# A new order for the steps of a two-stage attention and token-mixing kernel

## The chip, the cores and the metric

The kernel runs on one core of a Trainium2 chip. The metric is the time of one execution in microseconds on the device, as the median of several runs. All inputs and the output lie in the device's memory (DRAM) as float32.

## The reference

Two attentions stand one behind the other, and a token-mixing layer behind them. There are 8 batches of 8 heads, 576 tokens, 64 elements per head, and 32 packed queries per head.

```python
def sm_attn(qq, kk, vv):
    s = scale * np.matmul(qq, kk.transpose(0, 1, 3, 2))
    s = s - np.max(s, axis=-1, keepdims=True)
    a = np.exp(s)
    a = a / (np.sum(a, axis=-1, keepdims=True) + 1e-09)
    return np.matmul(a, vv)
p_packed = sm_attn(p, k, v)              # 32 packed rows per head
attn = sm_attn(q, p_packed, p_packed)    # 576 rows per head
...
x = attn.transpose(0, 2, 1, 3).reshape(B, S, H * D)      # (8, 576, 512)
wq = x @ w_q                             # (8, 576, 64)
wk = x @ w_k
W_tok = scale * np.einsum('bsd,btd->bst', wq, wk)
mixed = np.einsum('bst,btd->bsd', W_tok, x)
return np.maximum(mixed, 0.0) @ w_out
```

## The kernel before

Every batch is handled by the same chain of small steps, and the batches overlap: while TensorE multiplies for one batch, the other engines prepare the next. Each step is a short Python function that records a few instructions. The step's number is the batch, a second number its part. The steps of a batch in the order of the data:

- LD.k, LD.v, LD.q: loads from DRAM that convert to bfloat16, issued on GpSimd's queue. They all share one queue and land in its order.
- KT and QV (VectorE): 32x32 block transposes of k and q. S1 (TensorE): scores of the packed queries, 32 small matmuls. X1 (ScalarE): exponentials, two halves. TE (VectorE): transposes of them. PV (TensorE): the product with v, with a column of ones that gives the row sum.
- RC, PP, PT (VectorE): reciprocal, normalised packed values (`pp`), their transpose. QK (TensorE) and QKE, QD: packed values times the weights w_k and w_q.
- S2 (TensorE), X2 (ScalarE): scores of the 576 queries against the 32 packed rows and their exponentials, in chunks. RS, RR (VectorE): row sums and reciprocals. AM: the mask product, exponentials times reciprocal, on GpSimd or VectorE. Its part 2 is the last 128 columns of each half (256 in all), part 3 the first four tiles (1024), parts 0 and 1 two tiles each (512).
- AT, AE: transposes of the result on TensorE, and their copy out of PSUM. WKQ, WE: the products with QK's result. GM, GE, Y, YE, MX, MR: the mixing, through the 64-wide middle. RL, RLF, RLR: relu out of PSUM. OT, OH: the product with w_out, four matmuls of 512 columns for each tile of 128 tokens. OE, OEF, OEH: copies out of PSUM. ST, STF, STH: stores. OT.b.4 handles the 64 left-over tokens of two batches.
- WARM: matmuls of a tile of zeros into a PSUM bank that nobody reads. WARM.n has n units of 128 columns.

One string, `ORDER`, lists all steps. Each word names the step, behind `@` its engine (A ScalarE, V VectorE, P GpSimd, S SyncE; TensorE without a letter) and behind `=` the PSUM banks that it writes. A loop at the end of the kernel records them in that order:

```python
with tc.manual_schedule():
    for item in ORDER.split():
        name, _, bk = item.partition("=")
        name, _, eng = name.partition("@")
        f = name.split(".")
        ...
            steps[f[0]](*[int(z) for z in f[1:]], eng,
                        bk[0] if bk and len(bk) == 1 else bk)
```

So each engine runs its own steps in the order of the string, and waits at a step until what it reads, and the buffer or bank that it writes, are free. Nothing else orders the engines among each other. In particular nothing ties the mask product of one engine to that of another.

The lines that the texts below name: S1 L282, X1 L293, PV L315, RC L319, PP L323, QK L336, S2 L373, X2 L378, RS L394, RR L399, AM L405, AT L414 and L419, WKQ L441 and L446, GM L467, Y L477, MX L492, MR L498, RL and RLR L503 (ScalarE) and L505 (VectorE), OT L540, OH L580, WARM L619; all block transposes share L237, and copies L128 (ScalarE), L130 (GpSimd) and L132 (VectorE).

Of the kernel before, what the change touches and what calls it, by code (L numbers as in the profile page):

```python
# [13 lines left out]
LD.N0@A LD.N1@S SET.warm@V SET.v0@V SET.aT0@V SET.aT1@V SET.aT2@V SET.idf@V LD.W0@A LD.W1@S SET.tab@A LD.h0
LD.g0 LD.v0 LD.r0 LD.q0 LD.k1 NC.0@V PX.0@V NC.1@A PX.1@V SET.aff@P SET.idb@V SET.v3@P KT.0.0@V SET.mask@P
WC.1@P WC.0@P LD.k2 SET.v1@P LD.v1 SET.v2@P KT.0.1@V WARM.4=0 WARM.22.128=0 S1.0=0,1,2,3 X1.0.1@A TE.0.1@V
X1.0.0@A TE.0.0@V WARM.8=4 PV.0.0=4,5 PV.0.1 RC.0@V PP.0.0@V PP.0.1@V LD.q1 PT.0@V WARM.6=6 QK.0=6 QKE.0@A
QV.0.0@V QV.0.1@V QD.0@P WARM.4=7 S2.0.2=2,3 X2.0.2@A RS.0.2@V RR.0.2@V S2.0.0=0,1 LD.v2 S2.0.1=4,5 X2.0.0@A
RS.0.0@V RR.0.0@V X2.0.1@A RS.0.1@V RR.0.1@V AM.0.2@P WARM.6=7 AT.0.2=7 AE.0.2@A AM.0.0@P WARM.5=6 AT.0.0=6
KT.1.2@V AM.0.1@P WARM.3=2 AT.0.1=7 AE.0.1@A AE.0.0@V WKQ.0.0=2,3 WKQ.0.2 WE.0.0@A LD.q2 WKQ.0.1 KT.2.2@V  # L20
S1.1=0,1,4,5 WE.0.1@A GM.0=6 X1.1.0@A TE.1.0@V GE.0@A WARM.2=7 Y.0=2,3 YE.0@V S1.2=0,1,6,7 MR.0=2,3 X1.1.1@A
TE.1.1@V MX.0.0=4,5 X1.2.0@A LD.O PV.1.0=0,1 TE.2.0@V PV.1.1 X1.2.1@A TE.2.1@V RC.1@V LD.k3 PP.1.0@V PP.1.1@V
# [1 line left out]
RS.1.2@V RR.1.2@V S2.1.1=2,3 X2.1.0@A RS.1.0@V RR.1.0@V WARM.1=6 PV.2.0=6,7 PV.2.1 X2.1.1@A RS.1.1@V RC.2@V
LD.v3 QD.1@P AM.1.2@P AT.1.2=4 RR.1.1@V AM.1.0@P WARM.5=5 AT.1.0=5 AM.1.1@P LD.k4 PP.2.0@V AE.1.2@A PP.2.1@V
PT.2@V QK.2=4 AE.1.0@A QKE.2@A QD.2@P QV.2.2@V LD.q3 LD.v4 AT.1.1=0 AE.1.1@A WKQ.1.0=2,3 WKQ.1.2 WKQ.1.1
WE.1.0@V S2.2.2=6,7 WE.1.1@A X2.2.2@A S2.2.3=4,5 X2.2.3@A GM.1=1 OT.0.0=2,3 GE.1@V Y.1=6,7 OT.0.1 YE.1@A
RS.2.4@V OE.0.0@A MR.1=0,1 MX.1.1=4,5 RLR.1@A RR.2.4@V OT.0.2=6,7 LD.q4 OT.0.3 KT.3.2@V AM.2.3@P OE.0.1@V
RL.1.1@A S1.3=2,3,0,1 X1.3.0@A AM.2.2@P OT.1.4=4 TE.3.0@V LD.k5 AT.2.2=5 X1.3.1@A TE.3.1@V AT.2.3=2 AE.2.3@V
LD.v5 MX.1.0=6,7 AE.2.2@V PV.3.0=0,1 PV.3.1 OEF.1.4@A WKQ.2.0=2,3 WKQ.2.1 RC.3@V PP.3.1@V RL.1.0@A WKQ.2.2  # L30
WE.2.2@A OT.1.2=4,5 OT.1.3 PP.3.0@V PT.3@V QK.3=6 OE.1.1@A LD.q5 KT.4.2@V S1.4=0,1,2,3 GM.2=7 OT.1.0=4,5
X1.4.1@A LD.k6 GE.2@A QKE.3@V X1.4.0@A QV.3.2@V TE.4.1@V Y.2=2,3 YE.2@A S2.3.2=6,7 X2.3.2@A S2.3.3=0,1
X2.3.3@A MX.2.0=2,3 TE.4.0@V RL.2.0@A MR.2=6,7 RLR.2@V OT.1.1 MX.2.1=6,7 RL.2.1@A OE.1.0@A PV.4.0=0,1 QD.3@P
PV.4.1 RS.3.4@V RR.3.4@V LD.v6 AM.3.3@P AM.3.2@P RC.4@V OT.2.0=2,3 OT.2.1 LD.q6 OE.2.0@A PP.4.0@V PP.4.1@V
PT.4@V QK.4=6 AT.3.3=7 QV.4.2@V AT.3.2=0 AE.3.2@A LD.k7 S2.4.2=4,5 AE.3.3@V X2.4.2@A S2.4.3=2,3 X2.4.3@A
KT.5.2@V WKQ.3.0=0,1 WKQ.3.1 WKQ.3.2 RS.4.4@V RR.4.4@V QKE.4@A WE.3.2@A S1.5=4,5,2,3 X1.5.1@A LD.v7 TE.5.1@V
OT.2.2=6,7 AM.4.3@P QD.4@P AM.4.2@P GM.3=0 X1.5.0@A TE.5.0@V GE.3@A OT.2.3 Y.3=2,3 YE.3@V PV.5.0=4,5 PV.5.1
HOLD.v7 MR.3=0,1 RC.5@V PP.5.1@V OE.2.1@A MX.3.0=2,3 PP.5.0@V PT.5@V MX.3.1=6,7 RLR.3@A RL.3.0@A OT.3.4=0
RL.3.1@A AT.4.2=1 AE.4.2@A OEF.3.4@A QV.5.2@V AT.4.3=5 AE.4.3@V ST.1.4@P QK.5=4 QKE.5@V QD.5@P S2.5.2=2,3
X2.5.2@A KT.6.2@V S2.5.3=6,7 X2.5.3@A HA.5@P WKQ.4.0=0,1 WKQ.4.2 LD.q7 WKQ.4.1 WE.4.2@A OT.3.0=2,3  # L40
S1.6=4,5,6,7 X1.6.0@A GM.4=0 GE.4@V TE.6.0@V LD.r7 OT.3.1 X1.6.1@A TE.6.1@V Y.4=0,1 OE.3.0@A RS.5.4@V RR.5.4@V
PV.6.0=4,5 YE.4@A PV.6.1 MX.4.0=6,7 RC.6@V RL.4.0@A PP.6.0@V AM.5.3@P PP.6.1@V PT.6@V MX.4.1=2,3 AM.5.2@P
OT.3.2=0,1 OT.3.3 RL.4.1@A QK.6=4 QKE.6@A QV.6.2@V ST.2.1 S2.6.2=6,7 X2.6.2@A S2.6.3=2,3 ST.3.4 MR.4=4,5
X2.6.3@A OE.3.1@V RLR.4@V KT.7.2@V AT.5.2=6 AE.5.2@A AT.5.3=7 OT.4.0=0,1 OT.4.1 AE.5.3@A WKQ.5.0=4,5 WKQ.5.2
OE.4.0@A ST.0.8@P WKQ.5.1 RS.6.4@V WE.5.2@A RR.6.4@V ST.3.0 ST.4.0 ST.1.8@P S1.7=2,3,6,7 X1.7.1@A AM.6.3@V
OT.4.2=0,1 GM.5=4 TE.7.1@V OT.4.3 AT.6.3=5 X1.7.0@A TE.7.0@V GE.5@A OE.4.1@A AM.6.2@P AT.6.2=4 ST.2.0 Y.5=6,7
YE.5@A ST.3.1 PV.7.0=2,3 QV.7.1@V AE.6.3@V QV.7.0@V AE.6.2@A QD.6@P PV.7.1 RC.7@V PP.7.0@V PP.7.1@V PT.7@V
MR.5=0,1 RLR.5@A MX.5.1=6,7 RL.5.1@A MX.5.0=4,5 RL.5.0@V WKQ.6.0=0,1 WKQ.6.1 WKQ.6.2 WE.6.2@A OT.5.4=2
OEF.5.4@A S2.7.1=6,7 ST.5.4 GM.6=3 GE.6@V X2.7.1@A RS.7.1@V RR.7.1@V S2.7.2=0,1 X2.7.2@A S2.7.0=4,5 QK.7=2
X2.7.0@A RS.7.0@V RR.7.0@V Y.6=6,7 YE.6@A OT.5.2=0,1 MX.6.1=4,5 QKE.7@A MX.6.0=6,7 AM.7.1@P RS.7.2@V RR.7.2@V  # L50
MR.6=2,3 OT.5.3 RLR.6@V RL.6.0@V RL.6.1@A OE.5.1@A ST.4.1 AM.7.0@P OT.5.0=2,3 AM.7.2@P AT.7.0=4 AE.7.0@A
AT.7.1=5 AE.7.1@V AT.7.2=6 AE.7.2@V OT.6.2=0,1 OEF.6.2@A QD.7@P WKQ.7.0=4,5 WKQ.7.2 WKQ.7.1 WE.7.0@A WE.7.1@A
STF.6.2 OT.6.0=6,7 OT.6.1 GM.7=0 OE.6.0@V OT.5.1 OE.5.0@V ST.5.1 GE.7@A Y.7=4,5 OT.6.3 OEF.6.3@V ST.6.0
# [599 lines left out]
```

## Time and profile before

| | us |
|---|---|
| median of 3 runs | 104.29 |
| lowest, highest | 104.27, 104.53 |
| span of the profiled execution, first to last instruction | 102.8 |

| engine | busy us | share of the span |
|---|---|---|
| TensorE matmuls (PE) | 92.7 | 90% |
| TensorE weight loads (PEld, beside PE) | 54.6 | 53% |
| VectorE (DVE) | 73.7 | 72% |
| ScalarE (ACT) | 65.0 | 63% |
| GpSimd (POOL) | 51.8 | 50% |

The profile gives the profiled execution's span and no other time of it; the timed runs are 1.5 us longer than the span. A timeline row reads: start, duration, engine, line, operation, tile written <- tiles read, shape, count, and in brackets the idle time of the engine just before it and what ended that. A waits or groups row adds such instructions up. In the windows, the columns are the busy time of PE, PEld, DVE, ACT and POOL with their counts, the granted TensorE clock, the DMA engines' share and GB/s. Line numbers of the changed kernel are two lower, as the string has two lines less.

### The profile page before, as it was taken

To read this page: it belongs to the slowest core of one execution; us is meant where nothing else is said; L and a number is where in the kernel's file an instruction comes from. 1 tells how busy PE (TensorE), PEld (TensorE's weight loads), DVE (VectorE), ACT (ScalarE), POOL (GpSimd) and SP (SyncE) were. 2 spreads that over 40 slices of the span, in tenths; PEclk is the share of its full clock that TensorE was granted. 3 is DMA by queue.
4 is the path that set the end of the run, shared out by engine and by line. 5 is a ranking of instruction groups with operands and counts; after the bars stand their busy time and mean duration, and the time that the engine had idled before them with its cause. 6 is when DMAs were issued, how large, how long until landed. Compare 5 with 4: busy or idle time off the path is not lost.

```text
span 102.8 us, 3593 instructions
## 1 busy us (share of the span) xinstructions
PE 92.7 (90%) x1536; PEld 54.6 (53%) x1536; DVE 73.7 (72%) x140; ACT 65.0 (63%) x111; POOL 51.8 (50%) x81
## 2 busy tenths in 40 slices
...
PEclk9999999999999999999999999999999999999999
...
GB/s 9 249 230 207 213 210 213 207 209 213 205 211 207 212 211 210 213 205 212 211 212 207 211 213 204 217 211 203 255 262 409 411 410 408 418 345 264 335 364 160
DMA packets 13279, 25.13 MB, mean 244 GB/s; under 512 B 1040, under 2 KB 6416, under 8 KB 13008
## 3 DMA queue, kind: packets, MB, share of 16 engines
...
q8 instruction: 12, 0.20, 0.7%
...
## 4 chain that ended last, share of the span: by engine, by line
PE 49%; DMA 21%; DVE 8%; POOL 7%; ACT 6%; issue 3%; SPq 1%; DVEq 0%; POOLq 0%; ACTq 0%
PE ps L540 26%; DMA q_sb<-in_q_dram 13%; DMA o<-in_moe_w_q_dram 8%; PE ps L373 4%; POOL a L405 4%; PE ps L315 3%; ACT e1T L293 3%; PE ps L419 3%; PE ps L446 3%; DVE rs L394 2%; PE ps L441 2%; PE ps L467 2%; PE ps L282 2%; ACT e L378 1%; DVE qT L237 1%
## 5 line engine op out<-in xcount | busy, mean ns | idle before, releaser
L540 PE MATMUL ps<-wout,relu 128*128 128x512 bf16 x124 | 30.6, 380 | 0.0
L405 POOL TENSOR_TENSOR a<-e,rr 128x256 bf16<-128x256 f32 (+2 forms) x18 | 19.5, 1099 | 17.9 <-DVE rr L399 7.0
L619 PE MATMUL ps<-o 128*128 128x128 f32 (+3 forms) x76 | 19.5, 401 | 1.2 <-DVE o L135 1.2
L540 PEld LDWEIGHTS <-relu 128*128 128x128 bf16 x124 | 10.7, 98 | 11.7 <-issue 1.1
L128 ACT ACTIVATE o<-ps 128x1024 f32<-128x1024 f32 (+2 forms) x13 | 11.3, 871 | 5.4 <-PE ps L540 5.2
L619 PEld LDWEIGHTS ps<-o 128*128 128x128 f32 x76 | 11.3, 209 | 5.2 <-issue 3.6
L503 ACT ACTIVATE relu<-ps 128x1024 bf16<-128x1024 f32 (+1 forms) x14 | 13.0, 968 | 1.1 <-PE ps L492 1.1
L293 ACT ACTIVATE e1T<-ps 128x576 bf16<-128x576 f32 x16 | 9.8, 656 | 5.8 <-PE ps L282 5.2
L378 ACT ACTIVATE e<-ps 128x256 f32<-128x256 f32 (+2 forms) x19 | 11.2, 623 | 2.7 <-PE ps L373 2.5
L394 DVE TENSOR_REDUCE rs<-e 128x16 f32<-128x512 f32 (+2 forms) x13 | 10.9, 840 | 2.3 <-ACT e L378 2.2
L237 DVE STREAM_TRANSPOSE kT<-k_sb 128x1152 uint32<-128x1152 uint32 (+1 forms) x9 | 11.1, 1230 | 1.9 <-DMA k_sb<-in_k_dram 1.9
L173 POOL DMA_DIRECT2D v_sb<-in_v_dram x16 | 10.0, 628 | 4.0 <-DMA v_sb<-in_v_dram 1.6
L237 DVE STREAM_TRANSPOSE qT<-q_sb 128x1152 uint32<-128x1152 uint32 (+1 forms) x10 | 11.0, 1108 | 0.1
L132 DVE COPY o<-ps 128x1024 f32<-128x1024 f32 (+2 forms) x7 | 6.8, 977 | 5.3 <-PE ps L540 2.7
L237 DVE STREAM_TRANSPOSE e<-e1T 128x288 uint32<-128x288 uint32 x16 | 7.4, 468 | 3.1 <-ACT e1T L293 2.7
L128 ACT ACTIVATE aT<-ps 128x128 bf16<-128x128 f32 (+2 forms) x11 | 5.0, 465 | 5.7 <-PE ps L419 3.3
L128 ACT ACTIVATE wkq<-ps 128x448 bf16<-128x448 f32 (+1 forms) x10 | 7.2, 730 | 1.8 <-PE ps L446 1.7
L315 PE MATMUL ps<-v_sb,e 64*64 64x192 bf16 x288 | 7.5, 245 | 0.8 <-DVE e L237 0.5
L315 PEld LDWEIGHTS <-e 64*64 64x64 bf16 x288 | 5.9, 107 | 2.6 <-DVE e L237 2.1
L373 PEld LDWEIGHTS <-qT 64*128 64x128 bf16 x320 | 5.4, 94 | 2.8 <-DVE qT L237 1.7
L373 PE MATMUL ps<-ppT,qT 64*128 64x64 bf16 x320 | 6.6, 190 | 0.2 <-DVE qT L237 0.2
L446 PE MATMUL ps<-aT,pqk 128*128 128x256 bf16 (+1 forms) x48 | 6.8, 246 | 0.0
...
## 6 DMA issues: line engine op xcount, KB each, us to landing
...
```

What stands on the lines that cost most here:

```text
L128: nc.scalar.activation(o, i, COPY)
L173: nc.gpsimd.dma_start(v_bufs[b % NL][halves(i), 0:7:2], src)
L237: nc.vector.transpose(o, i)
L293: nc.scalar.activation(e1T[:, x], T["s1", b][x].rearrange("a c m -> a m c"), EXP, scale=scale)
L315: nc.tensor.matmul(T["pv", b][halves(cc), i], lhsT, rhs, start=n == 0, stop=n == R - 1, skip_group_check=True)
L373: nc.tensor.matmul(ps[:, y, t - t0, i], lhsT, rhs, start=e == 0, stop=e == 1)
L378: nc.scalar.activation(e2[:, t0:t1].rearrange("a t (i y n) -> a y (t i) n", i=2, y=2), T["s2", b, c].rearrange("a y t i n -> a y (t i) n") ...
L394: nc.vector.tensor_reduce(rs[:, t0 * H:t1 * H], src, axis=AX, op=ADD)
L405: e.tensor_tensor(a2[:, t0:t1].rearrange("a t i (u l) -> a (t i u) l", l=L), e2v(b, c), T["rr", b][:, t0 * H:t1 * H].to_broadcast((P, (t1 ...
L503: nc.scalar.activation(o, i, RELU)
L540: nc.tensor.matmul(ps, lhsT, wout[:, j, :], start=j == 0, stop=j == NJ - 1)
L619: nc.tensor.matmul(bank(int(bk), [w]), warm[:, 0:P], rhs, start=True, stop=True)
```

## The change

Only `ORDER` changes. Its words are the same up to the end of batch 0's first half (S1, PV, QK of batch 0), apart from bank numbers; behind that, the steps of batches 0 to 7 stand in another order, 39 steps change between ScalarE, VectorE and GpSimd, and many write other PSUM banks. Six mask products move from GpSimd to VectorE (AM.1.1, 2.3, 3.2, 4.2, 5.2, 7.2) beside the one that is there already (AM.6.3). The WARM units behind S1.1 grow from 11 to 17. Of the loads, LD.k4 is issued earlier, LD.q6 and LD.v6 change places.

```diff
-X1.2.0@A LD.O PV.1.0=0,1 TE.2.0@V PV.1.1 X1.2.1@A TE.2.1@V RC.1@V LD.k3 PP.1.0@V PP.1.1@V
-PT.1@V MX.0.1=6,7 QV.1.2@V RLR.0@A QK.1=2 QKE.1@V RL.0.0@A WARM.3=3 S2.1.2=4,5 S2.1.0=0,1 RL.0.1@A X2.1.2@A
...
+GE.0@A X1.2.1@A TE.2.1@V X1.2.0@A Y.0=0,1 TE.2.0@V YE.0@A LD.k3 WARM.3=6 MX.0.0=6,7 WARM.2=4 MX.0.1=4,5 QV.1.2@V
+PT.1@V WARM.3=2 RL.0.0@A S2.1.2=2,3 S2.1.1=0,1 X2.1.2@A X2.1.1@A S2.1.0=6,7 RS.1.2@V LD.v3 LD.k4 RR.1.2@V QK.1=2
```

The first place is on TensorE, around MX of batch 0 (L492 before, L490 after). The names are `y_0` for the result of YE.0, `o_1_86` for the tile of zeros of the fillers, `e1_1` for the exponentials of batch 1. Before:

```order
L498 MATMUL ps_61<-wkq_0_363,y_0_429 128x64
L492 LDWEIGHTS y_0_429
L492 MATMUL ps_61<-wkq_0_363,y_0_429 128x512
L492 LDWEIGHTS y_0_429
L492 MATMUL ps_61<-wkq_0_363,y_0_429 128x512
L315 LDWEIGHTS e1_1_197
L315 MATMUL ps_61<-v_sb1_66,e1_1_197 64x192
```

After:

```order
L475 MATMUL ps_61<-pp_0_243,g_0_496 64x128
L617 MATMUL ps_61<-o_1_86 128x384
L490 LDWEIGHTS y_0_508
L490 MATMUL ps_61<-wkq_0_363,y_0_508 128x512
L490 LDWEIGHTS y_0_508
L490 MATMUL ps_61<-wkq_0_363,y_0_508 128x512
L617 MATMUL ps_61<-o_1_86 128x256
```

MX.0.0 stood between MR.0 and PV.1; now it stands behind PV.1, Y.0 and a filler of 3 units, with another of 2 units behind it.

The second place is on VectorE and GpSimd, at the mask products of batch 4: `rr_285` is the reciprocal RR.4.4, `e_1_197` the transposed exponentials TE.5, `y_...` YE.3, `a_1_329` the mask product. VectorE before:

```order
L399 RECIPROCAL rr_285<-rs_283 128x40
L237 STREAM_TRANSPOSE e_1_197<-e1T_194 128x9x32 x2
L486 TENSOR_SCALAR y_429<-ps 128x256
L319 RECIPROCAL rec_241<-ps 128x2
L323 SCALAR_TENSOR_TENSOR pp_245<-ps,rec_241,mask 128x128 x2
```

VectorE after:

```order
L397 RECIPROCAL rr_285<-rs_283 128x40
L235 STREAM_TRANSPOSE e_1_197<-e1T_194 128x9x32 x2
L403 TENSOR_TENSOR a_1_329<-e_0_83,rr_285 128x256
L484 TENSOR_SCALAR y_508<-ps 128x256
L317 RECIPROCAL rec_241<-ps 128x2
L321 SCALAR_TENSOR_TENSOR pp_245<-ps,rec_241,mask 128x128 x2
```

GpSimd before:

```order
L173 DMA v_sb_68<-in_v_dram 64x4x576 x2
L405 TENSOR_TENSOR a_1_329<-e_0_83,rr_285 128x1024
L130 COPY pqk_264<-pqk_264 128x2x64
L405 TENSOR_TENSOR a_1_329<-e_0_83,rr_285 128x256
L559 DMA out_dram<-orem_866 128x512
```

GpSimd after:

```order
L174 DMA k_sb_72<-in_k_dram 128x2x1152
L403 TENSOR_TENSOR a_1_329<-e_0_83,rr_285 128x1024
L171 DMA v_sb_68<-in_v_dram 64x4x576 x2
L128 COPY pqk_264<-pqk_264 128x2x64
L386 TENSOR_TENSOR h_0_1411<-e_1_84 128x640
```

The small product AM.4.2 left GpSimd's queue for VectorE's, where it stands between TE.5.1 and YE.3; the loads of v7 went behind AM.4.3.

The third place is on VectorE at the start of batch 7: `rec_240` is RC.7, `pp_244` PP.7, `qT_268` QV.7, `ppT_250` PT.7, `aT_80` AE.6.3. Before:

```order
L237 STREAM_TRANSPOSE qT_268<-q_sb_76 128x2x288
L132 COPY aT_80<-ps 128x2x512
L237 STREAM_TRANSPOSE qT_268<-q_sb_76 128x2x288
L319 RECIPROCAL rec_240<-ps 128x2
L323 SCALAR_TENSOR_TENSOR pp_244<-ps,rec_240,mask 128x128 x2
L237 STREAM_TRANSPOSE ppT_250<-pp_244 128x128
```

After:

```order
L235 STREAM_TRANSPOSE qT_268<-q_sb_76 128x2x288
L130 COPY aT_80<-ps 128x2x512
L317 RECIPROCAL rec_240<-ps 128x2
L321 SCALAR_TENSOR_TENSOR pp_244<-ps,rec_240,mask 128x128
L503 TENSOR_SCALAR rem_632<-ps 128x4x64
L321 SCALAR_TENSOR_TENSOR pp_244<-ps,rec_240,mask 128x128
L235 STREAM_TRANSPOSE qT_268<-q_sb_76 128x2x288
L235 STREAM_TRANSPOSE ppT_250<-pp_244 128x128
```

RLR.5 went between the two PP, and QV.7.0 between them and PT.7.

More of the change, by code (lines that the diff above doesn't have):

```diff
@@ L13 @@
 ORDER = """
[L14 to L22, printed above, removed]
-PT.1@V MX.0.1=6,7 QV.1.2@V RLR.0@A QK.1=2 QKE.1@V RL.0.0@A WARM.3=3 S2.1.2=4,5 S2.1.0=0,1 RL.0.1@A X2.1.2@A
@@ L24 @@
[L24 to L53, printed above, removed]
@@ L54 @@
-STF.6.3 YE.7@A ST.5.0 MR.7=6,7 RLR.7@A MX.7.0=4,5 RLF.7.0.1@A RLF.7.0.0@V MX.7.1=2,3 RLF.7.1.0@A OT.7.4=0
-OEF.7.4@A ST.7.4 RLF.7.1.1@V OT.7.1=6 OEF.7.1@V OT.7.0=7 STF.7.1 OT.7.2=1 OEF.7.0@A OH.7.0=0 STF.7.0 OEF.7.2@A
-STF.7.2 OEH.7.0@V STH.7.0 OH.7.1=5 OEH.7.1@A STH.7.1@A
+LD.N0@A LD.N1@S SET.warm@V SET.v0@V SET.aT0@V SET.aT1@V SET.aT2@V SET.idf@V LD.W0@A LD.W1@S SET.tab@A LD.h0 LD.g0
+LD.v0 LD.r0 LD.q0 LD.k1 NC.0@V PX.0@V NC.1@A PX.1@V SET.aff@P SET.idb@V SET.v3@P KT.0.0@V SET.mask@P WC.1@P WC.0@P
@@ new lines @@
+LD.k2 SET.v1@P LD.v1 SET.v2@P KT.0.1@V WARM.4=0 WARM.22.128=0 S1.0=0,1,2,3 X1.0.1@A TE.0.1@V X1.0.0@A TE.0.0@V
+WARM.8=4 PV.0.0=4,5 PV.0.1 RC.0@V PP.0.0@V PP.0.1@V LD.q1 PT.0@V WARM.6=6 QK.0=0 QKE.0@A QV.0.0@V QV.0.1@V QD.0@P
+WARM.4=6 S2.0.2=6,7 X2.0.2@A RS.0.2@V RR.0.2@V S2.0.0=2,3 LD.v2 S2.0.1=4,5 X2.0.0@A RS.0.0@V RR.0.0@V X2.0.1@A
+RS.0.1@V RR.0.1@V AM.0.2@P WARM.6=1 AT.0.2=0 AE.0.2@A AM.0.0@P WARM.5=1 AT.0.0=0 KT.1.2@V AM.0.1@P WARM.3=1
+AT.0.1=1 AE.0.1@A AE.0.0@V WKQ.0.0=6,7 WKQ.0.2 WE.0.0@A LD.q2 WKQ.0.1 KT.2.2@V S1.1=2,3,4,5 X1.1.1@A WARM.3=0
```

32 lines of the change are left out of this document (added).

## The prediction

> **What bounds the kernel now.** I read the page's busy line first, then the windows, then TensorE's timeline for its waits, then the chain for what released them.
>
> ```profile
> span 102.8 us, 3593 instructions
> PE 92.7 (90%) x1536; PEld 54.6 (53%) x1536; DVE 73.7 (72%) x140; ACT 65.0 (63%) x111; POOL 51.8 (50%) x81
> PEclk9999999999999999999999999999999999999999
> 70.00:80.00 10.00, 10.00 (x196) 6.23 (x194) 9.83 (x14) 8.95 (x15) 5.38 (x6) 1.00 1.12 291
> 80.00:90.00 10.00, 9.96 (x150) 6.00 (x143) 7.44 (x18) 8.45 (x17) 2.86 (x4) 1.00 1.02 411
> ```
>
> TensorE is busy in 90% of the span, and in 19.96 of the 20 us from 70 to 90. Both kernels give it the same real work, at the full granted clock in every slice. The end therefore moves by what is put between that work: fillers (WARM matmuls on no data) and waits. The DMA column is full too (1.02 to 1.12), so a gain is limited from that side as well.
>
> From 38 us on TensorE waits noticeably only three times:
>
> ```profile
> 54.90 0.62 PE L419 MATMUL ps<-idb,a 128*128 128x128 bf16 x8 [0.44 <-POOL a L405]
> 57.66 0.48 PE L282 MATMUL ps<-kT,pT 32*32 32x288 bf16 x32 [0.32 <-DVE kT L237]
> 68.58 0.94 PE L315 MATMUL ps<-v_sb,e 64*64 64x192 bf16 x36 [0.47 <-DVE e L237]
> ```
>
> These are AT.3.3 waiting for its mask product on GpSimd (POOL), S1.5 for KT.5.2, and PV.6.0 for TE.6: 1.23 us together. More than that a new order can hardly win behind 38 us. Ahead of 38 us the reason is a load:
>
> ```profile
> 13.89 13.59 DMA q_sb<-in_q_dram
> 27.51 1.39 DVE qT L237
> 27.14 0.31 DVE L237 STREAM_TRANSPOSE ppT<-pp 128x128 uint32<-128x128 uint32 x1
> 28.94 0.78 PE L373 MATMUL ps<-ppT,qT 64*128 64x64 bf16 x40 [0.18 <-DVE qT L237]
> ```
>
> In the chain, q of batch 1 lands at 27.48, whatever the engines do; QV.1 follows at once, and S2.1 at 28.94. The change leaves that load and those ahead of it in place.
>
> **Part 1, from S1.1 to Y.1: 1.2 us lost.** The steps up to S1.1 (22.30) are the same. From there to Y.1 I follow both orders.
>
> ```profile
> 31.24 1.32 PE L619 MATMUL ps<-o 128*128 128x512 f32 x4
> 32.44 0.40 PE L419 MATMUL ps<-idb,a 128*128 128x128 bf16 x4
> 33.45 0.40 PE L419 MATMUL ps<-idb,a 128*128 128x128 bf16 x4 [0.18 <-POOL a L405]
> 34.97 0.78 PE L373 MATMUL ps<-ppT,qT 64*128 64x64 bf16 x40
> 36.94 0.25 PE L477 MATMUL ps<-pp,g 64*64 64x128 bf16 x4
> 37.12 1.04 PE L540 MATMUL ps<-wout,relu 128*128 128x512 bf16 x4
> 31.34 2.05 POOL L405 TENSOR_TENSOR a<-e,rr 128x512 bf16<-128x512 f32 x2 [0.22 <-DVE rr L399]
> 34.27 0.62 DVE L132 CAST wkq<-ps 128x448 bf16<-128x448 f32 x1 [0.21 <-PE ps L441]
> 36.19 0.29 DVE L132 CAST g<-ps 128x128 bf16<-128x128 f32 x1 [1.29 <-PE ps L467]
> ```
>
> A filler of 5 units takes 1.20 (31.24 to 32.44), so 0.24 a unit. Before has 11 units behind S1.1, the new order 17: 1.4 us more TensorE time, hidden only where it would have waited anyway. The landmarks:
> - S2.1: PT.1 (0.31) now stands behind QV.1.2 on VectorE (DVE), not ahead of it. QV.1.2 still starts at 27.51 and ends at 28.9, PT.1 at 29.2: S2.1 starts at 29.25, 0.3 later. The fillers around MX.0 end before that, and a wait of 0.3 stays.
> - Masks of batch 1: the sums of X2.1.1 and X2.1.0 now both precede RR.1.0, and RC.2 too. AM.1.0 on GpSimd (2.05 for two, so about 1.05) ends near 33.25 where it ended at 32.4. AM.1.1, now on VectorE, ends near 33.9. AT.1.1 moves from 33.45 to 33.95, and QK.2, which stood in its shadow, comes behind it.
> - S2.2 needs QV.2.2, now behind AM.1.1: 35.3 instead of 34.97. WKQ.1.1 follows S2.2, then OT.0.2 (0.87) while WE.1.1 (0.62 by VectorE's row) runs. GM.1 starts at 37.25.
> - Y.1 directly follows GM.1 on TensorE and needs GE.1 (0.29) from it, so TensorE idles 0.4. Before, OT.0.0 stood between. Y.1: 38.1 instead of 36.94.
>
> By Y.1 both have done the same real work (one OT of batch 0 each). So the new order is 1.2 behind there.
>
> **Part 2, the three waits go: 1.1 us won.** Between AT.3.2 and AT.3.3 now stands OT.2.1, ahead of S1.5 stands OT.2.2, ahead of PV.6.0 stand OT.3.2, MX.4 and OT.3.3. An OT is 0.87, more than each wait. Of 1.23 I count 1.1, as about 0.1 comes back in short waits for PSUM banks.
>
> **Part 3, mask products on two engines at once: 1.4 us lost.** Before has one on VectorE, AM.6.3; the change moves AM.1.1, 2.3, 3.2, 4.2, 5.2 and 7.2 there too.
>
> ```profile
> L405 POOL TENSOR_TENSOR a<-e,rr 128x256 bf16<-128x256 f32 x8 | 5.8, 731 | 4.5 <-DVE rr L399 4.5
> L405 POOL TENSOR_TENSOR a<-e,rr 128x1024 bf16<-128x1024 f32 x4 | 7.6, 1908 | 6.6 <-DVE rec L319 2.3 <-DVE rr L399 2.1 <-PE ps L492 1.5
> 76.23 0.40 DVE L399 RECIPROCAL rr<-rs 128x40 f32<-128x40 f32 x1
> 76.67 1.23 DVE L405 TENSOR_TENSOR a<-e,rr 128x1024 bf16<-128x1024 f32 x1
> 76.79 1.58 POOL L405 TENSOR_TENSOR a<-e,rr 128x256 bf16<-128x256 f32 x1 [3.22 <-DVE rr L399]
> 59.10 0.40 DVE L399 RECIPROCAL rr<-rs 128x40 f32<-128x40 f32 x1
> 59.65 1.91 POOL L405 TENSOR_TENSOR a<-e,rr 128x1024 bf16<-128x1024 f32 x1 [0.64 <-ACT e1T L293]
> L237 DVE STREAM_TRANSPOSE e<-e1T 128x288 uint32<-128x288 uint32 x16 | 7.4, 468 | 3.1 <-ACT e1T L293 2.7
> 60.49 0.43 DVE L486 TENSOR_SCALAR y<-ps 128x256 bf16<-128x256 f32 x1 [0.30 <-PE ps L477]
> ```
>
> VectorE's AM.6.3 ran from 76.67 to 77.90; GpSimd's small product, issued at 76.79, took 1.58 where the kind takes 0.73 in the mean (this one included), and ended 0.47 after VectorE's. So the one that came second stood until the first was done. The trace shows this with VectorE first only. With GpSimd first, VectorE's product costs between nothing and the rest of GpSimd's. I take the whole rest, by the one pair that there is, and VectorE's queue stands with it.
>
> The Trainium skill, "SBUF — State Buffer", section "SBUF: two separate sides", says that whichever of a two-input VectorE operation and a GpSimd one starts first keeps the shared ports for the whole instruction and the other fully blocks. The pair at 76.67 agrees; no row here shows GpSimd first. By that rule the total is the one forecast below, without it 1.4 less.
>
> Who is first: GpSimd starts 0.15 after the reciprocal ends (59.50 to 59.65), VectorE when its queue gets there.
> - AM.4.2 stands behind two TE transposes (2 x 0.47). GpSimd, whose loads are out of the way, starts AM.4.3 at +0.15 and ends at +2.06; AM.4.2 would have started at +0.94 and now stands 1.1. YE.3 (0.43) is queued behind it, and MR.3 waits for YE.3: +2.06 +0.35 (1.23 by a quarter gives 0.31, and a start) +0.43 = +2.85. TensorE is ready for MR.3 at about +1.9, after PV.5 (0.9) behind TE.5.1. Loss 1.0.
> - AM.5.2 stands behind one TE, and TE.6.1, for which PV.6 waits, behind it. TE.6.1 ends at +2.06 +0.35 +0.47 = +2.9, not at +1.3. How much of these 1.6 the OT and MX steps ahead of AT.5.2 cover is open: an estimate between 0 and 0.65 is lost; I take 0.4.
> - AM.3.2 comes 0.3 after its reciprocal (one PP ahead of it), GpSimd 0.15 plus its own start. GpSimd's product at 76.79 needed only 0.47 of its usual time after VectorE ended, so part of its start was done before: a near tie. First on VectorE costs nothing, first on GpSimd 1.5. I take nothing, and keep 1.5 for the range.
>
> **Part 4, batches 6 and 7: 1.1 us lost.**
>
> ```profile
> 77.67 1.03 PE L540 MATMUL ps<-wout,relu 128*128 128x512 bf16 x4
> 78.54 0.61 PE L419 MATMUL ps<-idb,a 128*128 128x128 bf16 x8
> 81.50 0.31 DVE L237 STREAM_TRANSPOSE ppT<-pp 128x128 uint32<-128x128 uint32 x1
> 80.01 0.76 DVE L237 STREAM_TRANSPOSE qT<-q_sb 128x576 uint32<-128x576 uint32 x1
> 82.55 0.41 PE L373 MATMUL ps<-ppT,qT 64*128 64x64 bf16 x16
> 94.31 1.08 ACT L503 ACTIVATE relu<-ps 128x512 bf16<-128x512 f32 x2
> ```
>
> - AT.6.2, whose product ends last (78.37 above), now goes ahead of GM.5 and AT.6.3, so TensorE gets to it 0.3 sooner than it got to AT.6.3 (78.54). And S2.6, the start of that chain, is one OT later than its cover. Loss 0.6.
> - PT.7 now stands behind RLR.5 (0.4) and QV.7.0 (0.76): 1.16 later after PV.7. Before, S2.7 started 0.74 after PT.7's end (81.81 to 82.55). Loss 0.4, part of it behind MX.5.1: 0.3.
> - The last four relus are now all on ScalarE (ACT), 1.08 for two, so 2.2, under OT.6.3 and OT.7.4 (1.7) and the last MX: 0 to 0.5, I take 0.2.
>
> **The other edits** come at nothing: bank numbers and some 30 evictions that change engine, of 0.3 to 1.2 us each, lie beside a TensorE that has other work, and a load issued later (v4, q4, k6) still has earlier ones ahead of it in its queue. Taken off that cover, each would cost its own duration at most.
>
> **The sum.** +1.2 -1.1 +1.4 +1.1 = +2.6 us on a span of 102.8, so 105.4. The median of the runs is 104.29; the 1.5 us around the profiled span I carry over unchanged: 106.9 us.
>
> **The rivals.**
> - Products only block where VectorE is first (part 3 at nothing): 105.5. For it: no row shows the other direction. Against: the row that there is shows a full stop, not a share. Chance 0.20.
> - AM.3.2 is caught as well: 108.4. Chance 0.13.
> - Faster: VectorE gets its product in first in every pair, because GpSimd comes to its own later than I count, with loads ahead of it. Then no transpose waits for a mask, TensorE has no wait left behind 38 us, and parts 2 to 4 give back the 1.23 and the smaller gaps (0.3 or so), against 1.2 at the start: -0.4, 103.9. It decides where TensorE's waits behind 38 us sum to less than 0.4. For it: GpSimd is only 50% busy and TensorE has long runs of OT as cover. Against: the rows at 59.65 and 76.79 show it starting 0.15 after the reciprocal. Chance 0.17.
> - The change is even (104.3): the start loses what the waits give back, with nothing else. Chance 0.08.
> - My forecast, 106.9, has the remaining 0.42, with 106.0 to 107.8 as its own range.
>
> The measurement can tell about 0.3% (0.3 us). Faster 0.17, same 0.08, slower 0.42 + 0.20 + 0.13 = 0.75. The range from 104.0 to 108.5 leaves out most of the faster case and the far end of AM.3.2.
>
> **What would show it.** Right: Y.1 near 38.1; a VectorE product of 256 columns that lasts or is preceded by over 1 us beside GpSimd's AM.4.3, with MR.3 waiting for YE.3; GpSimd's AM.6.2 again near 1.6, now with AT.6.2 waiting. Wrong: Y.1 before 37.3; small VectorE products of 0.35 with no idle time while GpSimd's run; or TensorE waits behind 38 us below 1 us in all.

## The result, and the profile after

The changed kernel takes 107.11 us (median of 4 runs, 106.95 to 107.22) against 104.28 us for the kernel before (4 runs on the same chip, 104.22 to 104.53). The ratio is 1.0265, with a 95% interval from 1.0244 to 1.0287: slower by 2.8 us. The forecast was 106.9 us. The profiled span grew by 2.5 us, from 102.8 to 105.3. Every execution that comes with its own span is 1.7 to 1.9 us longer than that span (107.06 for the 105.3 here). The median execution of before so has a span of about 102.5, an estimate from 104.28 less 1.8: the profiled one was one of its longer ones, and that is why the spans differ by less than the medians.

All ratios compare the means of fast runs; two kernels below also have one run each in a slower state (108.10 and 109.25), which only their medians include.

From the page of the changed kernel ("after" from here on), the busy line and the granted clock:

```profile
span 105.3 us, 3577 instructions
PE 94.6 (90%) x1524; PEld 56.3 (53%) x1540; DVE 75.2 (71%) x141; ACT 67.4 (64%) x116; POOL 48.1 (46%) x75
PEclk9999999999999999999999999999999999999999
```

TensorE has the full clock throughout, as before, so the time went into what stands between its real work and behind it. Its timeline in after shows where (the brackets hold the idle time and what ended it):

```profile
28.97 0.78 PE L371 MATMUL ps<-ppT,qT 64*128 64x64 bf16 x40
33.00 0.40 PE L417 MATMUL ps<-idb,a 128*128 128x128 bf16 x4 [0.33 <-POOL a L403]
33.55 0.40 PE L417 MATMUL ps<-idb,a 128*128 128x128 bf16 x4 [0.15 <-DVE a L403]
37.57 0.25 PE L475 MATMUL ps<-pp,g 64*64 64x128 bf16 x4 [0.37 <-ACT g L126]
61.97 0.23 PE L496 MATMUL ps<-wkq,y 64*128 64x64 bf16 x4 [0.93 <-DVE y L484]
71.70 0.23 PE L412 MATMUL ps<-idb,a 128*128 128x64 bf16 x2 [0.36 <-DVE a L403]
72.09 0.94 PE L313 MATMUL ps<-v_sb,e 64*64 64x192 bf16 x36 [0.15 <-DVE e L235]
80.05 0.23 PE L412 MATMUL ps<-idb,a 128*128 128x64 bf16 x2 [0.80 <-POOL a L403]
81.20 0.95 PE L313 MATMUL ps<-v_sb,e 64*64 64x192 bf16 x33
100.02 1.04 PE L578 MATMUL ps<-wout,relu 128*128 128x384 bf16 x8
```

These are S2.1, AT.1.0, AT.1.1, Y.1, MR.3, AT.5.2, PV.6, AT.6.2, PV.7 and OH.7. The waits of before at AT.3.3, S1.5 and PV.6 are gone or nearly so; MR.3, AT.5.2 and AT.6.2 wait instead. (Three matmuls of PV.7 stand just ahead of the row shown, the first at 81.09.) In the timeline of before the three landmarks that the prediction doesn't show are MR.3, PV.7 and OH.7:

```profile
61.12 0.23 PE L498 MATMUL ps<-wkq,y 64*128 64x64 bf16 x4
79.22 0.91 PE L315 MATMUL ps<-v_sb,e 64*64 64x192 bf16 x36
97.93 1.04 PE L580 MATMUL ps<-wout,relu 128*128 128x384 bf16 x8
```

At each of these (and at Y.1) TensorE has the same amount of real work behind it in both orders, so the difference is the lag of after: 0.63 us at Y.1, 0.85 at MR.3 (that step's own wait is 0.93, so after was 0.08 ahead of before until then), 1.9 to 2.0 at PV.7, 2.09 at OH.7, 2.5 at the end of the span.

Why MR.3 and AT.5.2 wait is on VectorE. Its timeline in after, around AM.3.2, AM.4.2 and AM.5.2:

```profile
52.41 0.41 DVE L403 TENSOR_TENSOR a<-e,rr 128x256 bf16<-128x256 f32 x1
58.83 0.40 DVE L397 RECIPROCAL rr<-rs 128x40 f32<-128x40 f32 x1
59.15 0.89 DVE L235 STREAM_TRANSPOSE e<-e1T 128x288 uint32<-128x288 uint32 x2
59.97 1.60 DVE L403 TENSOR_TENSOR a<-e,rr 128x256 bf16<-128x256 f32 x1
61.50 0.41 DVE L484 TENSOR_SCALAR y<-ps 128x256 bf16<-128x256 f32 x1
69.57 2.07 DVE L403 TENSOR_TENSOR a<-e,rr 128x256 bf16<-128x256 f32 x1
```

and GpSimd's mask products beside them:

```profile
52.48 2.12 POOL L403 TENSOR_TENSOR a<-e,rr 128x1024 bf16<-128x1024 f32 x1 [4.29 <-DVE rr L397]
59.38 1.91 POOL L403 TENSOR_TENSOR a<-e,rr 128x1024 bf16<-128x1024 f32 x1 [1.40 <-DVE rr L397]
69.45 1.91 POOL L403 TENSOR_TENSOR a<-e,rr 128x1024 bf16<-128x1024 f32 x1 [1.44 <-DVE rr L397]
78.41 1.58 POOL L403 TENSOR_TENSOR a<-e,rr 128x256 bf16<-128x256 f32 x1 [5.18 <-ACT o L126]
```

The same VectorE instruction takes 0.41 where it starts first (52.41, GpSimd 0.07 behind it) and 1.60 or 2.07 where GpSimd is already running. Both long ones end 0.28 after GpSimd's end (61.57 after 61.29, 71.64 after 71.36): VectorE's product was held until then.

### The profile page after: what moved, and what is told of

It reads as the page before. It is cut to its first block, busy times and chain, and to the rows that moved or that the text cites. A ratio compares the mean times of both kernels' runs of the same rounds, so it can differ in the third digit from the quotient of the medians.

```text
span 105.3 us, 3577 instructions
## 1 busy us (share of the span) xinstructions
PE 94.6 (90%) x1524; PEld 56.3 (53%) x1540; DVE 75.2 (71%) x141; ACT 67.4 (64%) x116; POOL 48.1 (46%) x75
## 4 chain that ended last, share of the span: by engine, by line
PE 57%; DVE 20%; ACT 12%; POOL 4%; issue 4%; DVEq 0%; POOLq 0%; ACTq 0%
PE ps L617 18%; PE ps L538 15%; DVE rs L392 4%; DVE kT L235 4%; POOL a L403 4%; PE ps L417 3%; PE ps L313 3%; PE ps L371 3%; ACT e1T L291 3%; ACT relu L501 3%; ACT o L126 3%; DVE a L403 2%; PE ps L444 2%; PE ps L490 2%; DVE e L235 2%
## 5 line engine op out<-in xcount | busy, mean ns | idle before, releaser
L538 PE MATMUL ps<-wout,relu 128*128 128x512 bf16 x111 | 29.6, 381 | 0.9 <-issue 0.3
L403 POOL TENSOR_TENSOR a<-e,rr 128x512 bf16<-128x512 f32 (+2 forms) x12 | 15.5, 1297 | 27.1 <-DVE rr L397 18.3
L617 PE MATMUL ps<-o 128*128 128x128 f32 (+3 forms) x80 | 22.6, 430 | 1.2 <-DVE o L133 1.2
L617 PEld LDWEIGHTS ps<-o 128*128 128x128 f32 x80 | 13.1, 229 | 6.0 <-issue 4.3
L126 ACT ACTIVATE o<-ps 128x1024 f32<-128x1024 f32 (+2 forms) x15 | 13.6, 904 | 3.8 <-PE ps L538 3.6
L501 ACT ACTIVATE relu<-ps 128x1024 bf16<-128x1024 f32 (+1 forms) x16 | 14.0, 923 | 1.0 <-PE ps L490 0.8
L313 PE MATMUL ps<-v_sb,e 64*64 64x192 bf16 x288 | 7.6, 245 | 0.6 <-DVE e L235 0.5
L403 DVE TENSOR_TENSOR a<-e,rr 128x256 bf16<-128x256 f32 (+2 forms) x7 | 8.0, 1142 | 0.1
L126 ACT ACTIVATE aT<-ps 128x128 bf16<-128x128 f32 (+1 forms) x10 | 4.0, 407 | 5.5 <-PE ps L417 3.0
L130 DVE COPY o<-ps 128x1024 f32<-128x1024 f32 (+2 forms) x5 | 4.1, 825 | 4.7 <-PE ps L538 3.5
L313 PEld LDWEIGHTS <-e 64*64 64x64 bf16 x288 | 6.0, 107 | 2.6 <-DVE e L235 2.3
L126 ACT ACTIVATE wkq<-ps 128x896 bf16<-128x896 f32 (+1 forms) x8 | 6.2, 778 | 1.6 <-PE ps L444 1.4
```

The lines of the kernel that those rows point to most:

```text
L126: nc.scalar.activation(o, i, COPY)
L313: nc.tensor.matmul(T["pv", b][halves(cc), i], lhsT, rhs, start=n == 0, stop=n == R - 1, skip_group_check=True)
L403: e.tensor_tensor(a2[:, t0:t1].rearrange("a t i (u l) -> a (t i u) l", l=L), e2v(b, c), T["rr", b][:, t0 * H:t1 * H].to_broadcast((P, (t1 ...
L501: nc.scalar.activation(o, i, RELU)
L538: nc.tensor.matmul(ps, lhsT, wout[:, j, :], start=j == 0, stop=j == NJ - 1)
L617: nc.tensor.matmul(bank(int(bk), [w]), warm[:, 0:P], rhs, start=True, stop=True)
```

## The experiments

All kernels were run beside the kernel before on the same chip, and ratios are against those runs. The edits show only the words around each change. The theory is the prediction's: on TensorE's path lie the start, the two mask products that GpSimd shuts out, and AT.6.2. The rivals are that the products are not the cause, or that what is won in one place is lost at the next.

**VectorE first.** AM.4.2 and AM.5.2 stay on VectorE but stand directly behind their reciprocals.

```diff
-RR.4.4@V TE.5.0@V X1.5.1@A TE.5.1@V
+RR.4.4@V AM.4.2@V TE.5.0@V X1.5.1@A TE.5.1@V
...
-PV.5.1 AM.4.2@V YE.3@V
+PV.5.1 YE.3@V
```

and AM.5.2 likewise behind RR.5.4.

> The changed order, with AM.4.2 and AM.5.2 still on VectorE but directly behind their reciprocals (RR.4.4, RR.5.4), ahead of the TE transposes. Theory A (whichever product starts first keeps the other out until it ends): AM.4.2 and AM.5.2 take about 0.4 us instead of 1.60 and 2.07, GpSimd's AM.4.3 and AM.5.3 get longer by 0.2 to 0.4, TensorE's wait before MR.3 (0.93) falls below 0.2 and those before AT.5.2 and PV.6 (0.51) below 0.2; the TE transposes come 0.4 later, which gives 0.1 to 0.4 back. Time 1.0 us less than the changed kernel: 106.1 (105.7 to 106.4). Theory B (a VectorE product beside one of GpSimd is slow, whichever starts first): AM.4.2 and AM.5.2 stay above 1 us, the time stays at 107.1. Theory C (these waits lie beside something later that is just as late, a load or a store): the waits go, the time stays within 0.3 of 107.1.

Measured: 105.98 us, ratio 1.012 (1.0085 to 1.0154). VectorE's AM.4.2 and GpSimd's AM.4.3 in this kernel, and the one wait that came instead, at PV.5, whose transposes now stand behind the product:

```profile
59.23 0.42 DVE L403 TENSOR_TENSOR a<-e,rr 128x256 bf16<-128x256 f32 x1
59.35 2.09 POOL L403 TENSOR_TENSOR a<-e,rr 128x1024 bf16<-128x1024 f32 x1 [1.39 <-DVE rr L397]
60.46 0.94 PE L313 MATMUL ps<-v_sb,e 64*64 64x192 bf16 x36 [0.43 <-DVE e L235]
```

The product is short again, GpSimd's runs 0.18 longer, and MR.3, AT.5.2 and PV.6 wait no more. This is theory A.

**Both on GpSimd.** The same two products go to GpSimd, in the same places.

```diff
-AM.4.2@V
+AM.4.2@P
-AM.5.2@V
+AM.5.2@P
```

> The changed order, with AM.4.2 and AM.5.2 on GpSimd, ahead of its AM.4.3 and AM.5.3, so that no VectorE product meets them. Theory A: they take 0.6 each on GpSimd, AM.4.3 and AM.5.3 end 0.6 later, which AT.4.3 and AT.5.3 have the time for; the waits before MR.3 and PV.6 go. Time 105.8 (105.4 to 106.2), a little below the kernel with VectorE first, as the TE transposes don't move. Theory B gives the same here. Theory C: 107.1.

Measured: 105.52 us, ratio 1.0094 (1.0068 to 1.012). GpSimd does each pair in one piece:

```profile
59.27 2.48 POOL L403 TENSOR_TENSOR a<-e,rr 128x256 bf16<-128x256 f32 x2 [1.39 <-DVE rr L397]
68.46 2.49 POOL L403 TENSOR_TENSOR a<-e,rr 128x256 bf16<-128x256 f32 x2 [1.46 <-DVE rr L397]
```

Of after's 2.65% this takes back 1.7 points. Behind 38 us only AT.6.2's wait is left.

**The collision alone, in the kernel before.** One step is moved, nothing else.

```diff
-AM.4.3@P QD.4@P AM.4.2@P GM.3=0 X1.5.0@A TE.5.0@V GE.3@A
+AM.4.3@P QD.4@P GM.3=0 X1.5.0@A TE.5.0@V AM.4.2@V GE.3@A
```

> Before with one step moved: AM.4.2 from GpSimd to VectorE, behind TE.5.1. Theory A (GpSimd's AM.4.3 is running by then and shuts VectorE out until it is done): AM.4.2 lasts 1.3 to 1.7 instead of 0.4, TensorE waits about 0.9 at MR.3, 105.2, ratio 1.007 to 1.010. Theory B (the wait of 0.93 in after comes from somewhere else in its order): VectorE's product takes about 0.4 there, MR.3 is no later, 104.3 or less, ratio 0.998 to 1.000.

Measured: 105.56 us, ratio 1.0113 (1.0091 to 1.0136), a little more than theory A has. In its timeline, VectorE's AM.4.2, GpSimd's AM.4.3 and TensorE's MR.3:

```profile
60.21 1.73 DVE L403 TENSOR_TENSOR a<-e,rr 128x256 bf16<-128x256 f32 x1
59.75 1.91 POOL L403 TENSOR_TENSOR a<-e,rr 128x1024 bf16<-128x1024 f32 x1 [0.83 <-ACT e1T L291]
62.33 0.23 PE L496 MATMUL ps<-wkq,y 64*128 64x64 bf16 x4 [1.05 <-DVE y L484]
```

The collision is shown by itself: one product of 0.4 us, put on the other engine behind the wrong neighbour, costs 1.2 us of the whole.

**AT.6.3 first.** AT.6.2 goes behind AT.6.3, and its copy AE.6.2 behind GE.5.

```diff
-X1.7.1@A AT.6.2=2 AM.6.3@V X1.7.0@A GM.5=3 AT.6.3=6 AE.6.2@A TE.7.1@V TE.7.0@V GE.5@A
+X1.7.1@A AM.6.3@V X1.7.0@A GM.5=3 AT.6.3=6 AT.6.2=2 TE.7.1@V TE.7.0@V GE.5@A AE.6.2@A
```

> The changed order, with AT.6.3 ahead of AT.6.2 on TensorE, and AE.6.2 behind GE.5 on ScalarE. The wait of 0.80 before AT.6.2 is for GpSimd's AM.6.2, which stands until VectorE's AM.6.3 is done and ends at 79.99. If that wait is on the path: GM.5 and AT.6.3 run in it, a rest of at most 0.15 stays, and the time falls by 0.5 to 0.8, to 106.4. If it is only exchanged for a later wait (AE.6.2 and PV.7's bank, or the stores at the end): within 0.3 of 107.1.

Measured: 106.82 us, ratio 1.020 (1.0158 to 1.0241). The wait of 0.80 is gone, a smaller one at MX.5 stands in its place:

```profile
81.93 0.39 PE L490 MATMUL ps<-wkq,y 64*128 64x512 bf16 x2 [0.26 <-ACT y L482]
```

The ratio is 0.65 points below after's, and the two intervals lie just apart (up to 1.0241 here, from 1.0244 in after). But the median is only 0.29 us below after's, and in the profiled execution OH.7 begins at 99.82, 0.2 sooner than in after. So most of the 0.80 came back behind it, and the two readings of the expectation are not told apart.

**The start of before.** The first attempt joined before's order up to Y.1 to after's rest. There OT.0.2 writes the banks of Y.1, and S1.3 those of OT.0.0, before these are read, so its YE.1 and OE.0.0 compute from other data, and its waits are not those of either order.

```diff
 GM.1=1 OT.0.0=2,3 GE.1@V Y.1=6,7
+OT.0.2=6,7 OT.0.3 YE.1@A MX.1.0=4,5
```

> The order of before up to Y.1 of batch 1 (with its 11 filler units), the changed order for all that is left. My part 1 (the new start loses 0.8 to 1.2 us): Y.1 comes at 36.9 instead of 37.6 and the time falls by 0.8 to 1.2, to about 106.1. The rival, that the new start costs nothing because batches 2 to 5 catch up on it (the loads and the waits behind 38 us absorb it): MR.3 and what follows stay where they are, 107.1.

Measured: 109.57 us, ratio 1.0465 (1.0426 to 1.0503). It says nothing on the question. Joined one step later, behind OE.0.0, no bank is written too early:

```diff
 Y.1=6,7 OT.0.1 YE.1@A RS.2.4@V OE.0.0@A
+OT.0.2=6,7 OT.0.3 MX.1.0=4,5 KT.3.2@V RR.2.4@V
```

> The order of before up to the copy OE.0.0 behind Y.1, and from there the order of after. Theory A (the new start is 0.6 to 1.2 us slower, as part 1 had it: 17 filler units where 11 stood, and the wait of Y.1 for GE.1): 106.0 to 106.5, ratio to before 1.015 to 1.020. Theory B (the start only looks slower; a load or a later wait takes up what it wins): as after, 107.1, ratio 1.026.

Measured: 108.41 us, ratio 1.04 (1.0332 to 1.0468): both theories missed. **The start of after with before's rest**, the mirror image:

```diff
 Y.1=2,3 OT.0.3 YE.1@A
+QD.2@P LD.v4 OT.0.0=2,3 OT.0.1 RS.2.4@V OE.0.0@A MR.1=0,1
```

> The mirror image: the order of after up to YE.1, and from there the order of before. Theory A: before plus 0.6 to 1.2 us, 104.9 to 105.5, ratio 1.006 to 1.012. Theory B: as before, 104.3, ratio 1.000.

Measured: 106.25 us, ratio 1.0188 (1.0135 to 1.024), more than theory A's 0.6 to 1.2 us. Its timeline shows Y.1 and two waits right behind the joint:

```profile
37.71 0.25 PE L475 MATMUL ps<-pp,g 64*64 64x128 bf16 x4 [0.37 <-ACT g L126]
41.77 0.75 PE L280 MATMUL ps<-kT,pT 32*32 32x288 bf16 x32 [0.73 <-ACT o L126]
42.96 1.02 PE L538 MATMUL ps<-wout,rem 128*128 128x512 bf16 x4 [0.45 <-ACT relu L501]
```

The joint itself costs 1.18 of the 1.95 us: at that place the two orders leave different copies unfinished. The remaining 0.8 is Y.1's lag (37.71 against 36.94). The start's price is therefore read from this row, not from the ratio; in the first of the pair, where Y.1 stands at 36.73, the joint's waits are larger still (0.57, 0.44 and 0.31).

**All four mended**: the start of before (joined as in the second attempt), both products on GpSimd, AT.6.3 first, and the stores ST.0.8 and ST.1.8 directly behind LD.r7.

```diff
-X2.7.0@A RL.5.1@V ST.0.8@P S2.7.1=0,1
+X2.7.0@A RL.5.1@V S2.7.1=0,1
...
-ST.5.4 ST.1.8@P WKQ.7.1
+ST.5.4 WKQ.7.1
...
-LD.r7 RL.4.0@A
+LD.r7 ST.0.8@P ST.1.8@P RL.4.0@A
```

> After with all four mended together: the start of before, AM.4.2 and AM.5.2 on GpSimd, AT.6.3 ahead of AT.6.2, the two stores early. Theory A (the four costs lie one behind the other on TensorE and add up): 107.1 - 0.8 (start) - 1.6 (the two products) - 0.7 (AT.6.2) - 0.3 (stores) = 103.7, ratio 0.995. Theory B (waits won in one place come back in another, at loads above all): 104.5 to 105.0, ratio 1.002 to 1.007.

Measured: 106.97 us, ratio 1.0212 (1.0125 to 1.0299); neither theory. The timeline shows the joint, and behind it PV.3 (L313), which takes 1.66 us where it takes 0.94 in the kernel with only the start of before:

```profile
40.85 0.48 PE L280 MATMUL ps<-kT,pT 32*32 32x288 bf16 x31 [0.57 <-ACT o L126]
41.77 0.39 PE L490 MATMUL ps<-wkq,y 64*128 64x512 bf16 x2 [0.43 <-ACT relu L501]
42.85 0.85 PE L417 MATMUL ps<-idb,a 128*128 128x128 bf16 x8 [0.31 <-ACT e1T L291]
43.74 1.66 PE L313 MATMUL ps<-v_sb,e 64*64 64x192 bf16 x36
```

The windows of this kernel (busy time of PE, PEld, DVE, ACT, POOL, then granted clock, DMA share, GB/s) name the reason:

```profile
39.99:43.00 3.01, 1.55 (x43) 0.85 (x42) 1.76 (x3) 3.01 (x5) 3.01 (x4) 1.00 1.12 212
43.00:46.50 3.50, 3.50 (x49) 2.39 (x48) 1.27 (x5) 1.27 (x3) 1.94 (x3) 0.51 1.14 208
```

After 3 us in which TensorE was busy for only half the time, it was granted half the clock for 3.4 us. Single runs point to what that does: 105.81 us at a mean clock of 0.996, 106.90 and 107.05 at 0.983 and 0.980; with only the start of before, 107.67 and 108.11 at 1.0, 108.83 and 108.70 at 0.984.

**Fewer fillers** in after.

```diff
-YE.0@A LD.k3 WARM.3=6 MX.0.0=6,7 WARM.2=4 MX.0.1=4,5 QV.1.2@V PT.1@V WARM.3=2
+YE.0@A LD.k3 MX.0.0=6,7 MX.0.1=4,5 QV.1.2@V PT.1@V
```

> After without three of its fillers, 8 units of the 17 behind S1.1: those around MX.0 (at 26.01, 27.17 and 28.12 in the trace of after). They fill the time until QV.1.2 is done with the load of q of batch 1. Theory A (the prediction's count: units beyond before's are TensorE time lost, 0.24 each): up to 1.4 us faster, 105.7, ratio 1.013. Theory B (they lie in the wait for that load and cost nothing; the start is slow for its masks and Y.1): 107.1, ratio 1.026. Theory C (they hold the granted clock up, as in the kernel with all four mended, where waits of 1.3 us in 3 were followed by 3.4 us at half clock): idle 2.4 us in 3.5, then half clock for about 3.4 us, 1 to 1.7 us slower, 108.1 to 108.8, ratio 1.036 to 1.043.

Measured: 107.36 us, ratio 1.0289 (1.0264 to 1.0314), not to be told from after. Theory A is out. The windows show theory C's mechanism, and the timeline that it was nearly paid for by the earlier start:

```profile
26.00:28.00 2.00, 0.61 (x4) 0.11 (x4) 2.00 (x4) 1.29 (x2) 0.71 (x1) 1.00 1.23 207
28.50:31.50 3.00, 3.00 (x84) 2.69 (x81) 1.88 (x4) 2.65 (x5) 0.90 (x2) 0.50 1.13 209
```

```profile
28.37 1.25 PE L371 MATMUL ps<-ppT,qT 64*128 64x64 bf16 x40 [1.45 <-DVE ppT L235]
```

S2.1 starts 0.6 sooner than in after, takes 1.25 instead of 0.78 at half clock, and the waits at AT.1.0 and AT.1.1 shrink to nothing; Y.1 comes at 37.79, 0.2 later, which is within the spread of the kernels that share after's order up to there (37.46 to 37.81). So the fillers stood in time that was idle anyway, and in the profiled execution without them the clock fell. A run without them that kept a clock of 1.0 took 107.33, no less than the 107.09 and 107.38 of those at 0.984, so the fall shows no price in the total here.

**The stores early**, alone: the two stores moved as in the diff above, the rest as in after.

> After, with the two stores ST.0.8 and ST.1.8 back directly behind LD.r7 on their queue, 11 and 17 us earlier. Theory A (the last 0.4 us of the loss lie behind TensorE: the last stores need 2.8 us to land instead of 2.5 because late stores stand ahead of them): 106.7 to 106.8, ratio 1.022 to 1.024. Theory B (the last store's own time varies, whatever was stored earlier): as after, 107.1.

Measured: 106.92 us, ratio 1.0247 (1.02 to 1.0293). From OH.7 to the span's end it takes 4.96 us (100.24 to 105.2) where after takes 5.28, as theory A has it, and the last two stores take 2.3 and 2.5 us to land instead of 2.6 and 2.8; but the total does not differ from after's beyond its interval, so this stays unproved.

**Three mended, with after's own start**, without a joint: both products on GpSimd, AT.6.3 first, the stores early.

> After with three mended and its own start kept, so without a seam: AM.4.2 and AM.5.2 on GpSimd, AT.6.3 ahead of AT.6.2, the two stores early. Theory A (the costs add up, and what spoiled the kernel with all four mended were the waits at its seam and the half clock behind them): 107.1 - 1.6 - 0.7 - 0.2 = 104.6, ratio 1.002 to 1.005. Theory B (the gains do not add): 105.0 to 105.5, ratio 1.007 to 1.012.

**And Y.1's wait filled**:

```diff
-GM.1=1 GE.1@A Y.1=2,3 OT.0.3 YE.1@A MX.1.0=4,5 RS.2.4@V KT.3.2@V RR.2.4@V OT.0.0=0,1
+GM.1=1 OT.0.3 GE.1@A Y.1=2,3 YE.1@A OT.0.0=0,1 MX.1.0=4,5 RS.2.4@V KT.3.2@V RR.2.4@V
```

> The same, and OT.0.3 between GM.1 and Y.1, OT.0.0 ahead of MX.1.0, so that TensorE has work while GE.1 and YE.1 run. Theory A (Y.1's wait of 0.37 is lost time): 0.3 to 0.4 us below the run with three mended, 104.2, ratio 0.998 to 1.001. Theory B (S1.3, whose banks OT.0.3 frees, and the loads behind it set the pace there): no difference to the run with three mended.

Measured: 105.72 us, ratio 1.0132 (1.0107 to 1.0157), and 105.55 us, ratio 1.0118 (1.0099 to 1.0138). This is near theory B in both: the three mends together are no better than the two products alone (1.0094), and filling Y.1's wait changes the total by nothing that can be told. Yet in the second of these TensorE has no wait over 0.35 us behind 25 us, and it begins OH.7 ahead of before's 97.93:

```profile
97.66 1.04 PE L578 MATMUL ps<-wout,relu 128*128 128x384 bf16 x8
```

From there to the end of the span it takes 6.1 us, before 4.9, after 5.3. The last two stores of before, with their size and the time from issue to landing:

```profile
out_dram<-o SPq DMA_DIRECT2D x1, 192.0 KB, 2.5
out_dram<-o ACTq DMA_DIRECT2D x1, 64.0 KB, 2.0
```

and those of the kernel with Y.1's wait filled, although they are issued 0.2 to 0.3 us sooner (99.1 against 99.3 and 99.4):

```profile
out_dram<-o SPq DMA_DIRECT2D x1, 192.0 KB, 3.5
out_dram<-o ACTq DMA_DIRECT2D x1, 64.0 KB, 3.7
```

The windows of before, with the last two columns the DMA engines' share and GB/s:

```profile
75.00:100.00 25.00, 23.87 (x320) 13.34 (x318) 17.82 (x31) 17.49 (x33) 4.67 (x6) 1.00 0.96 364
100.00:101.50 1.50, 0.00 (x0) 0.00 (x0) 0.00 (x0) 0.00 (x0) 0.00 (x0) 1.00 0.97 340
101.50:102.80 1.30, 0.00 (x0) 0.00 (x0) 0.00 (x0) 0.00 (x0) 0.00 (x0) 1.00 0.00 0
```

and those of the kernel with Y.1's wait filled:

```profile
75.00:100.00 25.00, 23.40 (x310) 12.63 (x308) 16.10 (x31) 18.35 (x34) 4.40 (x5) 1.00 1.00 367
100.00:101.50 1.50, 0.00 (x0) 0.00 (x0) 0.00 (x0) 0.00 (x0) 0.00 (x0) 1.00 0.86 307
101.50:102.80 1.30, 0.00 (x0) 0.00 (x0) 0.00 (x0) 0.00 (x0) 0.00 (x0) 0.54 0.11 38
```

From 75 to 100 us both move the same, with the DMA engines full, and both have 0.51 MB left. Before moves it by 101.5 us; in the other kernel the share falls to 0.86 and then to 0.11, which may mean that a few of the DMA engines are still at work when the rest are done. What TensorE wins here, the last stores give back. In after's order they tend to take longer the sooner TensorE is done: 2.6 and 2.8 us in after (OH.7 at 100.02), 2.7 and 2.9 with both products on GpSimd (98.21), 3.1 and 3.3 with three mended (98.58), 3.5 and 3.7 here (97.66). That fits an end bound by the transfers. Why the last bytes take longer here than in before is not shown.

The early stores may have a price as well. In the kernel with three mended, the first load of q of batch 7 takes 7.76 us, and TensorE waits 0.47 for a copy that stands behind its transpose on VectorE:

```profile
72.07 7.76 DMA q_sb<-in_q_dram
81.26 0.29 PE L439 MATMUL ps<-pqk,aT 128*128 128x64 bf16 x4 [0.47 <-DVE aT L130]
```

With after's start this load takes 7.2 to 7.8 us in the three kernels with the stores early, and 5.3 to 6.8 in the five with them late. But with all four mended, where they are early too, it takes 4.9, so this stays open.

No version beats the kernel before. Which of the moved loads and stores makes the end longer was not separated by a run.

## Why the prediction was right

The direction, the place and the total held; of the terms some were too large, and one was missing.

- **Part 1, sized too high** (+1.2; measured +0.63 at Y.1). The step that failed is the timing of the chain to Y.1. PT.1's wait of 0.3 did not show in this execution, because the load of q landed early and QV.1.2 started at 27.04, although the prediction had this load land at 27.48 whatever the engines do; in the run with the stores early it started at 27.58, about as in before (27.51), S2.1 waited 0.32, and Y.1 stood at 37.81, a lag of 0.87. The rest is AM.1.1 and S2.2, which came 0.4 and 0.5 earlier than worked out. Over all traces that share after's order up to there, Y.1 begins at 37.46 to 37.81. Y.1's own wait was 0.37 (0.4 forecast). That the six more units are mostly hidden was right (shown by the run with fewer fillers).
- **Part 2** (-1.1). AT.3.3's and S1.5's waits, 0.76 together, are won: the lag falls from 0.63 to -0.08 before MR.3's wait. PV.6's 0.47 is lost again to the mask product in front of it.
- **Part 3** (+1.4). MR.3 waits 0.93 (1.0 forecast), AT.5.2 and PV.6 0.51 together (0.4), AM.3.2 was first on VectorE, by 0.06 to 0.07 us in every trace that has it there, and cost TensorE nothing: the near tie, for which the range kept 1.5 us, fell the way that was taken. Taking the two collisions away brought 1.4 to 1.7 points of the ratio, and the one collision put into the kernel before cost 1.2 us: the mechanism and its price are shown. That makes up half or more of the 2.8 us; the other terms are read from rows, and no run settles their price. The rival by which GpSimd does not block has fallen, and so has the faster one, in which VectorE is first in every pair. The Trainium skill, "SBUF — State Buffer", section "SBUF: two separate sides", states this exclusion for either order; both orders are now in the traces, and agree.
- **Part 4, its terms mixed** (+1.1). AT.6.2 waited 0.80, more than the 0.6, though taking that wait away moved OH.7 by only 0.2. PT.7 cost nothing (0.3 forecast): S2.7 started at 84.70 behind MX.5, after PT.7 was done at 84.31, and the four relus on ScalarE made TensorE wait nowhere (0.2 forecast).
- **Missing**: from OH.7 to the end after needs 0.4 us more than before. The prediction called the DMA column full and then put no term for it into the sum. Another 0.4 between the landmarks, 0.2 to 0.3 of it between MR.3 and PV.7, belongs to no wait that the trace names.

By the waits the sum is 0.63 - 0.71 + 0.93 + 0.51 - 0.47 + 0.80 = 1.7, with the 0.8 of the last point 2.5, against 2.6 forecast. That the total came so near is in part luck, with errors of both signs: 0.9 us too much in parts 1 and 4, 0.8 that was not in the sum. The 1.5 us carried over from span to time were too little as well, since every execution with its own span shows 1.7 to 1.9; with 1.8 the same sum would have given 107.2. And the terms of the faster rival (1.2 - 1.23 - 0.3) make -0.3, not its -0.4.
